# A list-scheduled attention and feed-forward kernel: new assumed durations and due times, plain reads for the unsplit products

## The chip, the cores and the metric

The kernel runs on one core of a Trainium2 chip. The metric is the time of one execution in microseconds (us), taken on the device; the median of some runs is compared. Engines are named as in the profile: PE is TensorE's matmuls, PEld its weight loads, DVE VectorE, ACT ScalarE, POOL GpSimd, SP SyncE, whose queue issues nearly all DMAs here.

## The reference

Eight batches of eight heads, 576 positions, head size 64; 32 packed rows per head read keys and values first, and the queries then read the packed rows. The attention's output, 4608 tokens by 512, goes through an ELU feed-forward of width 2048.

```python
def sm_attn(qq, kk, vv):
    s = scale * np.matmul(qq, kk.transpose(0, 1, 3, 2))
    s = s - np.max(s, axis=-1, keepdims=True)
    a = np.exp(s)
    a = a / (np.sum(a, axis=-1, keepdims=True) + 1e-09)
    return np.matmul(a, vv)
p_packed = sm_attn(p, k, v)                  # (8, 8, 32, 64)
out = sm_attn(q, p_packed, p_packed)         # (8, 8, 576, 64)
x = out.transpose(0, 2, 1, 3).reshape(B * S, H * D)
h = x @ w_in                                 # w_in: 512 x 2048
g = np.where(h > 0.0, h, np.exp(np.minimum(h, 0.0)) - 1.0)
return g @ w_out                             # w_out: 2048 x 512
```

## The kernel before, in words

The kernel never forms x: since x = a @ p_packed, it multiplies p_packed by w_in first (tile `m`, `mstep`, line 814) and then the softmax weights `a` by `m` (lines 1049, 1311, 1318).

Work comes in **visits**: one batch, one of two windows of its tokens (256 or 320 columns), and a run of the 16 slices f of the hidden width. One slice of a visit is: product h on PE; `relu` and `exp` on ACT (1326 and 1332 or 1061 and 1064); `elu` on DVE (1335 or 1056), on the own 256 columns into `e`, on a window's odd 64 columns into `hb`, which is sent to DRAM and worked off at the end; a high part `g` (a cast, line 313) and the low rest (1349) of the result; and the product with w_out, on PE (1417 to 1420). Precise products are made from high and low halves in three passes at float32r. Only batches 0 and 1, for the first four slices, use one float32 product with nothing split (`h_whole`, line 1311); such a matmul stands in the trace as two records, and the order of the program shows it once. `in_turn` reads an operand's two halves alternately, one element of each; the host has ordered queries and w_out to suit.

From batch 2's second window on, the output product takes two slices at once in Strassen's form (`strassen_pair`): seven products of 256 columns in three passes each (21 matmuls of 256 columns, some against sums of w_out blocks that are loaded again from DRAM as `sw`), with sums of blocks on DVE (1131), a cast of 896 columns on ACT and its rest on DVE (1140). A pair that stands in `S_PLAINS` is made plainly instead: 12 matmuls of 512 columns (or their like in halves), 512-column cast and rest, no sums and no `sw`.

The weights come as 64-bit words and are **converted** in the first part of the run: for each of 32 slices of 512 KB a load into one of three `raw` buffers, two steps on ACT (`field` and `tail`, line 343), two on DVE (`size` 361, `signed` 371), and for w_out a cast and a rest (385).

All this is recorded as operations (`op`) with an urgency, the engines that can do it, an assumed duration on each, what it needs, and the buffers that it takes. `schedule()` then walks a clock of its own: whenever an engine is free, the most urgent ready operation goes to it. What comes out is only the **order** of the instructions on each engine; on the chip the engines follow it and wait for semaphores. SP's queue runs in order too, so a store that waits holds up the loads behind it. Urgencies are the number of the slice in the order of visits, less a lead: `LI` and `LO` for the conversion of w_in and w_out, `LM` for m, `T_ATT...` for six steps of a batch's attention, `TM...` for its m, `T_SL` for the loads of `sw`. `lag` is time that the walk adds after an operation before its result counts.

Of the kernel before, what the change touches and what calls it, by code (L numbers as in the profile page):

```python
# [14 lines left out]
AF = mybir.ActivationFunctionType  # L15
# [5 lines left out]
def packed_attention_elu_ffn(  # L21
# [29 lines left out]
    G = 2  # L51
# [28 lines left out]
    ]  # L80
    T_ATT = [11.5, 7.0, 12.0, 17.0, 11.5, 18.0]
    T_ATT1 = [-20.0, -19, -16.0, -3.0, -18.5, -9.5]
    LI = 5.0
    LO = 2.5
    LM = 2.0
    LOOK = 4.0
    TM = [22.0, 27.0, 34.5, 25.5]
    FIRST = "q i3 o2 i2 i0 v k i1 o0".split()
    T_S2 = -4.0
    STAY = 9  # L90
    SWITCH = 0.105
# [3 lines left out]
    T_WS = 21  # L95
    T_AS = 3
    S_PLAIN = []
    S_PLAINS = {
        (2, 0): [7], (2, 1): [0], (3, 0): [1], (3, 1): [0], (4, 0): [0], (4, 1): [1],
        (5, 0): [0], (5, 1): [0], (6, 0): [], (6, 1): [1, 7],  # L100
    }
    T_SW7 = 27
    T_ATTS = {3: [-4, 2, -1.0, 7, 13.0, 21.5], 4: [-1.5, 7, 13.5, 3.0, 12.0, 24.0], 5: [-3.0, -2, -8.5, -5.5, 14.5, 28.0], 6: [7, 9, 13.5, 1.5, 13.0, 24.5], 7: [-3.5, -6, -5, 7.5, 14.5, 22.0]}
    TMS = {3: [19, 29, 30.0, 30.5], 4: [22, 19.5, 26.0, 27.0], 5: [10.5, 29, 29.0, 31.0], 6: [23, 18.5, 26.0, 24.0], 7: [16.5, 35, 30.0, 31.0]}
    T_RL = 20.5
    T_RX = 1.5
    T_HS = 12.0
    S_FIRST = (2, 1)
    T_SW = 13.5
    T_SL = 10.0  # L110
    T_SE = 16.0
    LOOK_S = 5.5
# [66 lines left out]
    def schedule():  # L179
# [8 lines left out]
        todo = sorted(ops, key=lambda o: (o.prio, o.n))  # L188
        idle_at = {e: 0.0 for e in GAP}
        now, out, mode, converted = 0.0, [], None, 0  # L190
        conv = set(conv_ops)

        def engine_for(o):

            if o.wait or o.ready > now:
                return None
            for r in {id(b.ring): b.ring for b in o.take}.values():
                if not r.grant([b for b in o.take if b.ring is r], now):
                    return None

            spare = 2.0 * (converted < len(conv_ops))
            e = min(o.on, key=lambda e: max(idle_at[e], now) + o.on[e] + spare * (e == "DVE"))
            return e if idle_at[e] <= now else None
# [128 lines left out]
    def weights(f, first, prio):  # L332
# [57 lines left out]
        t = FIRST.index(name) - 60 if name in FIRST else prio - 8  # L390
        ld = op(t, {"DMA": 1.45}, load, take=[raw])
        x = op(prio, {"ACT": 0.66, "DVE": 0.42}, field, [ld], take=[mi_b], use=[raw])
        y = op(prio, {"ACT": 0.66, "DVE": 0.42}, tail, [ld], take=[rd_b], use=[raw])
        y = op(prio, {"DVE": 0.69}, size, [x, y], use=[mi_b, rd_b])
# [27 lines left out]
    def attention(b, ts):  # L422
# [85 lines left out]
        for name, fn, bufs, t in (  # L508
            ("k", load_k, k_b, ts[0] - 6), ("v", load_v, v_b, ts[0] - 5), ("q", load_q, q_b, ts[0] - 3),
        ):  # L510
            lds[name] = []
            if b == 0:
                t = FIRST.index(name) - 60
            for n, x in enumerate(bufs):
                prev_ld = op(
                    t, {"DMA": (3.3 if b < 3 else 3.8) / len(bufs)}, lambda e, fn=fn, n=n: fn(e, n),
                    take=[x] + ([p_b] if (name, n) == ("k", 0) else []), after=[prev_ld],
                    lag=1.5 * (b > 2),
                )
                lds[name].append(prev_ld)  # L520
# [84 lines left out]
        if b < S_FIRST[0] + 1:  # L605
            o1 = op(t, {"PE": 1.0}, s1, ld_k, take=ps1 + e1s, use=[p_b] + k_b, after=[free], mode=1)
            for g in range(G):
# [66 lines left out]

        o = op(ts[2], {"PE": 1.28}, pv, ld_v + tr_done, take=[ps, pp_b], use=v_b + e1T, mode=2)
        done = []
        for g in range(G):
            def norm(e, g=g, ps=ps):
                if e == "ACT":
                    nc.scalar.mul(pp_b.t[:, g, :], ps.t[:, g, :D], sv["ri"][:, g:g + 1])  # L680
                else:
                    nc.vector.tensor_scalar(
                        out=pp_b.t[:, g, :], in0=ps.t[:, g, :D], scalar1=sv["ri"][:, g:g + 1],
                        scalar2=None, op0=ALU.mult,
                    )

            done.append(op(
                ts[2], {"ACT": 0.25, "DVE": 0.27}, norm, [o, o5] + done,
                use=[ps, pp_b],
            ))  # L690
# [327 lines left out]
    def strassen_pair(i, b, win, f):  # L1018
# [57 lines left out]
        elif not half:  # L1076
            ps_b, h_b = banks(1), Buf(R["h"], lambda: None)
            x = op(
                i, {"PE": 0.714 * 2}, lambda e: [h_mm(ps_b.t[:, n * 2 * P:(n + 1) * 2 * P], n) for n in range(2)],
                need, take=[ps_b, h_b], use=m_b + [st.a], after=[run["h"]],  # L1080
# [8 lines left out]
        else:  # L1089
            done = []  # L1090
            for n in range(2):
                ps_b, h_b = banks(1), Buf(R["h"], lambda: None)
                e_b = ring_tile("e", work, [P, HT + 2 * P], F32, "e")
                x = op(
                    i + n, {"PE": 0.885}, lambda e, n=n, ps_b=ps_b: h_mm(ps_b.t[:, :n_tok], n),
                    need, take=[ps_b, h_b], use=m_b + [st.a], after=[run["h"]],
# [102 lines left out]
        for a, group in zip(acc, groups):  # L1199
# [14 lines left out]
            ns = [y[0] for _, y, _ in group if y[0] is not None]  # L1214
            cost = 1.386 if plain else 0.355 * len(group)
            run["out"] = op(
# [12 lines left out]
        if last:  # L1229
# [33 lines left out]
            q = i - T_SE  # L1263
            y = op(q, {"ACT": 0.37, "DVE": 0.4}, first, [acc[0].last], take=[part], use=acc[:1])
            y = op(q, {"DVE": 0.42}, add1, [y], use=[part, acc[0]])
# [19 lines left out]
    for i, (b, win, f) in enumerate(order):  # L1285
# [38 lines left out]

        def relu(e, ps_b=ps_b, e_b=e_b, n_tok=n_tok):
# [7 lines left out]

        def elu(out, cs, e_b=e_b, ps_b=ps_b):
# [22 lines left out]
        need_a = a_done[0 if (b % 2, win) == (0, 0) else 1]  # L1357
        cost = (1.07 if long else 0.87) if h_whole else (0.885 if long else 0.714)
        x1 = op(
# [37 lines left out]
        def out_mm(e, one=slice(0, 1), i=i, f=f, g_b=g_b, acc=acc, first=first, final=final, g_whole=g_whole):  # L1397
# [24 lines left out]
        prev_out = run["out"] = op(  # L1422
            i + LOOK, {"PE": (0.9 if g_whole else 0.693) * n_t}, out_mm,
            last + [w_split.get(f) if not g_whole and f < F_PLAIN else w_ready[False, f]]
# [5 lines left out]
        if final:  # L1430
            t0 = b * S + cols.start + HT * odd
            rows = [[t0, t0 + P], [t0 + P, t0 + 2 * P]]
            if i == len(order) - 1:

                outs = [prev_out, op(
                    i + LOOK, {"PE": 0.693}, lambda e: out_mm(e, slice(1, 2)), after=[prev_out],
                    use=[g_b] + acc,
# [89 lines left out]
```

## Time and profile before

| | us |
|---|---|
| Median of 3 runs (lowest, highest) | 694.3 (693.08, 696.58) |
| The profiled execution's own time | 692.21 |
| Its span, first to last instruction | 690.4 |
| PE busy in it | 656.0 |
| DVE busy in it | 589.3 |
| ACT busy in it | 452.6 |

The span is what the trace covers; 1.8 us of that execution lie around it. A busy PE is one with a matmul in its pipeline, so a PE that waits briefly between two matmuls still counts as busy.

### The profile page before, as it was taken

The numbers are of one execution on the slowest core, as the hardware profiler recorded it, in microseconds if no ns is written. First come the engines' busy times: TensorE is split into PE (matmuls) and PEld (weight loads), VectorE is DVE, ScalarE is ACT, GpSimd is POOL, SyncE is SP. The second block draws the span as 40 slices with busy tenths as digits, with TensorE's granted clock in tenths as the row PEclk, the third lists the DMA queues.
The fourth block names the chain that finished last, engine by engine and source line by source line (L and its number), as shares of the span: only waits on it lengthen the run. The fifth ranks groups of instructions, "written<-read, shape, count | busy, mean of one in ns | idle before, by whom it ended". The sixth has DMA issues, their size and how long they took to land.

```text
span 690.4 us, 15992 instructions
## 1 busy us (share of the span) xinstructions
PE 656.0 (95%) x6013; PEld 566.8 (82%) x6013; DVE 589.3 (85%) x1324; ACT 452.6 (66%) x897; POOL 18.4 (3%) x26
## 2 busy tenths in 40 slices
PE   7589998899999999999999999999999999999996
PEld 3356777677778879898879988898899988999996
DVE  4689888799999698878987898779998998878975
ACT  5678999975767467666565556665665666555541
POOL 0000011111121000000000000000000000000000
PEclk9899999999999999999999999999999999999999
DMA  9846578739578716879779976788789878676873
GB/s 324 301 131 230 167 226 211 163 94 280 163 201 227 274 40 204 276 229 332 248 225 319 309 246 209 244 275 314 248 281 328 282 228 247 208 219 179 282 230 129
DMA packets 99052, 160.95 MB, mean 233 GB/s; under 512 B 25760, under 2 KB 34976, under 8 KB 98720
## 3 DMA queue, kind: packets, MB, share of 16 engines
q1 hardware_dynamic: 96096, 154.70, 69.1%
q0 software_dynamic: 2880, 5.24, 5.0%
q8 instruction: 47, 0.77, 0.4%
q14 instruction: 29, 0.24, 0.1%
HBM read 132.64 MB, written 27.26 MB: 232 GB/s over the span
## 4 chain that ended last, share of the span: by engine, by line
PE 56%; DVE 24%; ACT 9%; DMA 7%; issue 3%; SPq 0%; DVEq 0%; ACTq 0%
PE psum L1205 29%; PE psum L1049 15%; DVE g L1140 3%; PE psum L814 2%; DVE m_lo L827 2%; DMA raw<-in_w_in 2%; ACT g L313 2%; DMA raw<-in_w_out 2%; DVE e L1335 2%; PE psum L1318 2%; DVE w L1131 2%; DVE w L1056 2%; DVE g L1349 1%; PE psum L1311 1%; PE psum L1417 1%
## 5 line engine op out<-in xcount | busy, mean ns | idle before, releaser
L1205 PE MATMUL psum<-sw,g 128*128 128x256 f32 x1140 | 165.9, 276 | 0.0
L1205 PEld LDWEIGHTS psum<-sw,g 128*128 128x128 f32 x1140 | 146.1, 192 | 8.8 <-issue 5.3
L313 ACT CAST g<-w 128x896 fp32r<-128x896 f32 (+1 forms) x88 | 79.8, 907 | 48.0 <-DVE w L1131 25.9
L1140 DVE TENSOR_TENSOR g<-w,g 128x896 fp32r<-128x896 f32 (+1 forms) x88 | 91.6, 1041 | 21.9 <-ACT g L313 21.7
L1049 PE MATMUL psum<-a_hi,m_hi 128*128 128x320 f32 (+1 forms) x352 | 104.6, 297 | 1.7 <-DVE hb L1056 0.7
L1049 PE MATMUL psum<-a_lo,m_hi 128*128 128x320 f32 (+1 forms) x352 | 101.4, 288 | 0.0
L1049 PE MATMUL psum<-a_hi,m_lo 128*128 128x320 f32 (+1 forms) x352 | 101.4, 288 | 0.0
L1131 DVE TENSOR_TENSOR w<-w 128x128 f32<-128x128 f32 (+1 forms) x237 | 79.0, 333 | 6.0
L1205 PE MATMUL psum<-wo_a,g 128*128 128x256 f32 (+1 forms) x510 | 82.7, 293 | 0.8 <-DVE hb L1056 0.6
L1049 PEld LDWEIGHTS psum<-a_hi,m_hi 128*128 128x128 f32 x352 | 67.0, 190 | 9.4 <-ACT e L1064 2.4
L1205 PEld LDWEIGHTS psum<-wo_a,g 128*128 128x128 f32 x510 | 69.9, 191 | 5.7 <-issue 2.0
L1061 ACT ACTIVATE e<-psum 128x320 f32<-128x320 f32 x96 | 41.5, 435 | 46.9 <-PE psum L1049 45.2
L1205 PE MATMUL psum<-wo_b,g 128*128 128x256 f32 (+1 forms) x477 | 71.6, 278 | 0.0
L1049 PEld LDWEIGHTS psum<-a_lo,m_hi 128*128 128x128 f32 x352 | 67.1, 191 | 0.2
L1049 PEld LDWEIGHTS psum<-a_hi,m_lo 128*128 128x128 f32 x352 | 67.0, 190 | 0.0
L1205 PEld LDWEIGHTS psum<-wo_b,g 128*128 128x128 f32 x477 | 62.2, 192 | 4.1 <-issue 3.9
L1056 DVE SCALAR_TENSOR_TENSOR w<-e,psum 128x256 f32<-128x256 f32 x96 | 39.7, 413 | 12.5 <-ACT e L1064 12.3
L1061 ACT ACTIVATE w<-psum 128x512 f32<-128x512 f32 x40 | 23.9, 598 | 40.2 <-PE psum L1049 21.1
L1064 ACT ACTIVATE e<-e 128x320 f32<-128x320 f32 x96 | 44.8, 471 | 2.6
L1326 ACT ACTIVATE e<-psum 128x256 f32<-128x256 f32 (+1 forms) x80 | 32.9, 412 | 19.1 <-PE psum L1318 14.4
L1318 PE MATMUL psum<-a_hi,m_hi 128*128 128x256 f32 (+1 forms) x128 | 38.0, 297 | 4.9 <-DVE hb L1335 2.2
L814 PE MATMUL psum<-w_in_sb,ppT 64*32 64x512 f32 (+1 forms) x640 | 37.2, 524 | 3.8 <-DVE w_in_sb L371 2.9
(123 smaller groups left out, 1284.5 us busy)
## 6 DMA issues: line engine op xcount, KB each, us to landing
sw<-sw_dram SPq DMA_DIRECT2D x316, 256.0 KB, 4.0
raw<-in_w_in SPq DMA_DIRECT2D x16, 512.0 KB, 4.4
raw<-in_w_out SPq DMA_DIRECT2D x16, 512.0 KB, 4.6
kvq<-in_v SPq DMA_DIRECT2D x16, 512.0 KB, 5.4
out<-part SPq DMA_DIRECT2D x32, 256.0 KB, 3.7
sw_dram<-sw SPq DMA_DIRECT2D x32, 256.0 KB, 3.7
kvq<-in_kT SPq DMA_DIRECT2D x14, 576.0 KB, 5.2
kvq<-in_qT SPq DMA_DIRECT2D x14, 576.0 KB, 6.5
```

The lines of the kernel that those rows point to most:

```text
L313: (nc.scalar.copy if e == "ACT" else nc.vector.tensor_copy)(out=out, in_=in_)
L814: nc.tensor.matmul(ps.t[cols_of(pair), g, :w], lhsT=st.ppT.t[rows_of(g), pair, :], rhs=w_in_sb[rows_of(g), pair, c * FC + part * w:c * FC ...
L827: nc.vector.tensor_tensor(out=m_b[1].t[:, :, fs], in0=ps.t[:, :, :w], in1=m_b[0].t[:, :, fs].bitcast(F32), op=ALU.subtract,)
L1049: nc.tensor.matmul(ps, lhsT=m_b[p].t[:, g, o:o + P], rhs=in_turn(st.a.t[q][:, g, cols]), start=(n == 0), stop=(n == 3 * G - 1),)
L1056: nc.vector.scalar_tensor_tensor(out=out, in0=e_, scalar=-1.0, in1=ps, op0=ALU.add, op1=ALU.max)
L1061: nc.scalar.activation(out=out, in_=ps, func=AF.Relu, scale=-1.0)
L1064: nc.scalar.activation(out=x, in_=x, func=AF.Exp, scale=-1.0)
L1131: nc.vector.tensor_tensor(out=out, in0=x, in1=y, op=o)
L1140: nc.vector.tensor_tensor(out=g_b.all[:, 7 * P:(7 + b1 - b0) * P], in0=blocks(b0, b1), in1=g_b.all[:, :(b1 - b0) * P].bitcast(F32), op=ALU ...
L1205: nc.tensor.matmul(a.t[:, at * H:(at + rhs.shape[1]) * H], lhsT=operand(blk, p), rhs=rhs, start=new and n == k == 0, stop=a.final == (u, m ...
L1318: nc.tensor.matmul(ps_b.t[:, :n_tok], lhsT=m_b[x].t[:, g, o:o + P], rhs=in_turn(st.a.t[y][:, g, cols]), start=(n == 0), stop=(n == 3 * G - 1),
L1326: nc.scalar.activation(out=e_b.t[:, :n_tok], in_=ps_b.t[:, :n_tok], func=AF.Relu, scale=-1.0)
```

## The change

It replaces numbers that only `schedule()` reads: assumed durations (the 320-column product h from 0.885 to 0.817 us, a group of an output product from 0.693 to 0.649, `field` and `tail` from 0.66 to 0.68 and 0.71), and a `lag` of 1.8 us for weight loads and of 1.5 us for the loads of batches 1 and 2, so that the walk counts their data as there later. It replaces all leads, the order of the first nine loads (`FIRST`), and the pairs made plainly: of those listed in `S_PLAINS` for Strassen windows 17 instead of 9. Last, the unsplit products of line 1311 read their operand in one piece instead of in turn; relu and elu then read PSUM by halves in turn, so that what they write has the same order as before.

```diff
-    LI = 5.0
-    LO = 2.5
-    LM = 2.0
+    LAG_W = 1.8
+    SPARE = 1.375
+    LI = 10.75
+    LO = 3.625
+    LM = 4.5
...
-    FIRST = "q i3 o2 i2 i0 v k i1 o0".split()
+    FIRST = "i3 q k i1 o2 i2 v i0 o0".split()
...
-        (5, 0): [0], (5, 1): [0], (6, 0): [], (6, 1): [1, 7],
+        (6, 0): [6],
+        (6, 1): [0, 1, 5, 6, 7],
...
-        ld = op(t, {"DMA": 1.45}, load, take=[raw])
+        ld = op(t, {"DMA": 1.5}, load, take=[raw], lag=0.0 if t < -55 else LAG_W)
...
-                    lag=1.5 * (b > 2),
+                    lag=1.5 * (b > 0),
...
-                        rhs=in_turn(st.af.t[:, g, cols]), start=(g == 0), stop=(g == G - 1),
+                        rhs=st.af.t[:, g, cols], start=(g == 0), stop=(g == G - 1),
...
+        def pairs(x, h_whole=h_whole):
+            return x.rearrange("p (i m) -> p i m", m=2) if h_whole else x
...
+            return x.rearrange("p (m i) -> p i m", m=2)[:, cs.start // 2:cs.stop // 2]
...
-                out=e_b.t[:, :n_tok], in_=ps_b.t[:, :n_tok], func=AF.Relu, scale=-1.0
+                out=pairs(e_b.t[:, :n_tok]), in_=h(slice(0, n_tok)), func=AF.Relu, scale=-1.0
...
-                out=out, in0=e_b.t[:, cs], scalar=-1.0, in1=ps_b.t[:, cs], op0=ALU.add, op1=ALU.max
+                out=pairs(out), in0=pairs(e_b.t[:, cs]), scalar=-1.0, in1=h(cs),
+                op0=ALU.add, op1=ALU.max,
```

What the new numbers do to the order is seen at three places. The first is SP's queue after the queries of batch 1 (`kvq<-in_qT`); `raw` are weight loads, `out<-part` the first stores of the output. Before:

```order
L502 DMA kvq<-in_qT 128x4x288 x2
L348 DMA raw<-in_w_in 128x1024
L1466 DMA out<-part 128x512
L1003 DMA rest_dram<-hb 256x1x64
```

And now (line 348 has become 371, 1466 has become 1500, 1003 has become 1026):

```order
L525 DMA kvq<-in_qT 128x4x288 x2
L371 DMA raw<-in_w_in 128x1024 x2
L371 DMA raw<-in_w_out 128x1024
L1026 DMA rest_dram<-hb 256x1x64
L1500 DMA out<-part 128x512
```

Three weight loads instead of one stand ahead of the first store.

The second is ACT's queue at the same time, where the visit of batch 0's long window begins (`e<-psum 128x320` is its first relu). Before:

```order
L313 CAST g<-e 128x256
L1332 ACTIVATE e<-e 128x256
L313 CAST a_hi<-k 128x2x288
L737 ACTIVATE tmp<-tmp 128x576
L1326 ACTIVATE e<-psum 128x320
L1332 ACTIVATE e<-e 128x320
L313 CAST g<-e 128x256 x2
```

And now (313 has become 336, 343 has become 366, 737 has become 760, 1326 and 1332 have become 1359 and 1365):

```order
L1365 ACTIVATE e<-e 128x256
L1359 ACTIVATE e<-psum 128x320
L1365 ACTIVATE e<-e 128x320
L336 CAST g<-e 128x256
L366 ACTIVATE mi<-raw 128x512
L366 ACTIVATE rd<-raw 128x512
L336 CAST g<-e 128x256
```

A weight's two conversion steps now stand among the casts of that visit. Counted over the whole order, 28 conversion steps stand ahead of the ninth relu where 21 did, 32 for 28 ahead of the 13th, 40 for 38 ahead of the 21st, 59 for 61 ahead of the 37th; all 64 stand ahead of the 41st in both.

The third is PE's queue in batch 3, second window, third pair, one of the eight that are now plain. Before, after the pair's last h matmul:

```order
L1205 MATMUL psum<-wo_a,g 128x256 x3
L1205 MATMUL psum<-sw,g 128x256 x3
L814 MATMUL psum<-w_in_sb,ppT 32x512 x8
L1205 MATMUL psum<-sw,g 128x256 x6
L1205 MATMUL psum<-wo_a,g 128x256 x6
L1205 MATMUL psum<-sw,g 128x256 x3
```

And now (1205 has become 1228):

```order
L1228 MATMUL psum<-wo_a,g 128x512 x12
```

21 matmuls of 256 columns are 12 of 512, and none reads `sw`. Counted over the program, PE's 256-column output matmuls are 144 fewer and its 512-column ones 84 more; DVE's sums (1131) are 24 fewer and 8 of its rests are 512 columns wide for 896; SP issues 32 loads of `sw` fewer. ACT's count of conversion steps is the same. Two more moves are told in words: batch 1's first scores (line 531, now 554) stand between the two halves of batch 0's first m on PE instead of behind both, and batch 2's first scores and their transposes stand some 65 and 35 us of PE work earlier. The last 100 rows of PE's and DVE's queues hold the same kinds of work as before.

## Rows read from the trace of the kernel before

**Rows 1.** The page: each engine's busy time in us, share of the span, and instructions.

```profile
PE 656.0 (95%) x6013; PEld 566.8 (82%) x6013; DVE 589.3 (85%) x1324; ACT 452.6 (66%) x897; POOL 18.4 (3%) x26
```

**Rows 2.** Stretches: length, PE, PEld, DVE, ACT, POOL busy (records), clock, DMA share, GB/s.

```profile
0.00:20.00 20.00, 13.93 (x169) 7.21 (x177) 8.50 (x17) 11.09 (x22) 0.70 (x6) 0.91 0.92 334
20.00:40.00 20.00, 12.77 (x209) 7.37 (x194) 16.52 (x35) 15.36 (x35) 0.00 (x0) 0.83 0.75 254
45.00:50.00 5.00, 5.00 (x34) 3.48 (x34) 4.97 (x12) 3.56 (x9) 0.00 (x0) 1.00 0.00 0
90.00:100.00 10.00, 8.98 (x48) 7.15 (x47) 8.34 (x19) 9.94 (x23) 1.35 (x2) 1.00 0.83 244
120.00:130.00 10.00, 7.32 (x42) 6.00 (x42) 7.44 (x17) 8.56 (x21) 1.76 (x2) 1.00 0.91 246
320.00:360.00 40.00, 38.77 (x386) 32.98 (x386) 38.85 (x70) 23.99 (x37) 0.00 (x0) 1.00 0.78 255
```

**Rows 3.** The same view, 40 to 240 us as one stretch.

```profile
40.00:240.00 200.00, 188.62 (x1486) 148.42 (x1485) 178.27 (x420) 154.14 (x364) 17.75 (x20) 1.00 0.70 197
```

**Rows 4.** The chain that ended last, pieces of it: start, length, what.

```profile
10.50 10.06 DMA raw<-in_w_in
...
370.44 2.59 PE psum L1205 x12
...
668.28 14.75 PE psum L1205 x132
```

**Rows 5.** TensorE's waits, 0 to 40 us: for what, us in all, times, longest.

```profile
PE psum L642 <- ACT tmp L555: 5.1, 3, 2.3
PE psum L814 <- DVE w_in_sb L371: 2.9, 1, 2.9
```

**Rows 6.** SyncE's timeline: start, length, line, DMA.

```profile
38.27 0.56 SPq L348 DMA_DIRECT2D raw<-in_w_in  x1
53.40 0.35 SPq L1466 DMA_DIRECT2D out<-part  x1
```

**Rows 7.** SyncE's longest wait from 36 to 70 us: us in all, times, longest.

```profile
SPq L1466 <- ACT g L313: 14.9, 1, 14.9
```

**Rows 8.** TensorE's waits, 40 to 240 us.

```profile
PE psum L1318 <- DVE hb L1335: 2.2, 5, 0.7
```

**Rows 9.** TensorE's waits, 240 to 600 us.

```profile
PE psum L572 <- DVE m_lo L827: 1.3, 2, 1.1
```

**Rows 10.** VectorE's groups by line and shape: busy us, mean ns, idle before.

```profile
L1140 DVE TENSOR_TENSOR g<-w,g 128x896 fp32r<-128x896 f32 x79 | 85.5, 1082 | 21.1 <-ACT g L313 20.9
L1131 DVE TENSOR_TENSOR w<-w 128x128 f32<-128x128 f32 x158 | 45.4, 287 | 3.2
...
L1131 DVE TENSOR_TENSOR w<-w 128x256 f32<-128x256 f32 x79 | 33.6, 425 | 2.7
...
L361 DVE SCALAR_TENSOR_TENSOR mi<-mi,rd 128x512 uint32<-128x512 uint32 x32 | 22.0, 689 | 12.5 <-ACT rd L343 11.6 <-ACT mi L343 0.4
...
L371 DVE SCALAR_TENSOR_TENSOR mi<-raw,mi 128x512 uint32<-128x512 uint32 x16 | 12.0, 747 | 0.0
...
L1140 DVE TENSOR_TENSOR g<-w,g 128x512 fp32r<-128x512 f32 x9 | 6.2, 683 | 0.8 <-ACT g L313 0.8
```

**Rows 11.** TensorE's timeline: start, length, line, tiles, shape, records.

```profile
43.27 0.67 PE L814 MATMUL psum<-w_in_sb,ppT 64*32 64x256 f32 x16
...
49.83 1.51 PE L1311 MATMUL psum<-k,m_hi 128*128 128x320 f32 x4
...
70.42 1.24 PE L1311 MATMUL psum<-q,m_hi 128*128 128x256 f32 x4
...
204.02 1.09 PE L814 MATMUL psum<-w_in_sb,ppT 64*32 64x512 f32 x16
```

**Rows 12.** ScalarE's groups, two of them: busy us, mean ns, idle before.

```profile
L1064 ACT ACTIVATE w<-w 128x512 f32<-128x512 f32 x40 | 25.3, 632 | 1.0
...
L343 ACT ACTIVATE mi<-raw 128x512 f32<-128x512 f32 x32 | 24.4, 764 | 10.0 <-DMA raw<-in_w_in 7.2 <-DMA raw<-in_w_out 2.6
```

More of the change, by code (lines that the diff above doesn't have):

```diff
@@ L189, in schedule @@
         idle_at = {e: 0.0 for e in GAP}
+        idle_at["DMA"] = 0.7
         now, out, mode, converted = 0.0, [], None, 0
@@ L390, in weights @@
         t = FIRST.index(name) - 60 if name in FIRST else prio - 8
-        ld = op(t, {"DMA": 1.45}, load, take=[raw])
-        x = op(prio, {"ACT": 0.66, "DVE": 0.42}, field, [ld], take=[mi_b], use=[raw])
-        y = op(prio, {"ACT": 0.66, "DVE": 0.42}, tail, [ld], take=[rd_b], use=[raw])
+        ld = op(t, {"DMA": 1.5}, load, take=[raw], lag=0.0 if t < -55 else LAG_W)
+        x = op(prio, {"ACT": 0.68, "DVE": 0.42}, field, [ld], take=[mi_b], use=[raw])
+        y = op(prio, {"ACT": 0.71, "DVE": 0.42}, tail, [ld], take=[rd_b], use=[raw])
         y = op(prio, {"DVE": 0.69}, size, [x, y], use=[mi_b, rd_b])
@@ L605, in attention @@
         if b < S_FIRST[0] + 1:
-            o1 = op(t, {"PE": 1.0}, s1, ld_k, take=ps1 + e1s, use=[p_b] + k_b, after=[free], mode=1)
+            o1 = op(t, {"PE": 1.15}, s1, ld_k, take=ps1 + e1s, use=[p_b] + k_b, after=[free], mode=1)
             for g in range(G):
@@ L673, in pv @@
                         )
-        o = op(ts[2], {"PE": 1.28}, pv, ld_v + tr_done, take=[ps, pp_b], use=v_b + e1T, mode=2)
+        o = op(ts[2], {"PE": 1.36}, pv, ld_v + tr_done, take=[ps, pp_b], use=v_b + e1T, mode=2)
         done = []
@@ L687, in attention @@
             done.append(op(
-                ts[2], {"ACT": 0.25, "DVE": 0.27}, norm, [o, o5] + done,
+                ts[2], {"ACT": 0.31, "DVE": 0.27}, norm, [o, o5] + done,
                 use=[ps, pp_b],
@@ L1214, in strassen_pair @@
             ns = [y[0] for _, y, _ in group if y[0] is not None]
-            cost = 1.386 if plain else 0.355 * len(group)
+            cost = 1.3 if plain else 0.335 * len(group)
             run["out"] = op(
@@ L1263, in strassen_pair @@
             q = i - T_SE
-            y = op(q, {"ACT": 0.37, "DVE": 0.4}, first, [acc[0].last], take=[part], use=acc[:1])
+            y = op(q, {"ACT": 0.45, "DVE": 0.4}, first, [acc[0].last], take=[part], use=acc[:1])
             y = op(q, {"DVE": 0.42}, add1, [y], use=[part, acc[0]])
@@ L1332, in ex, with elu @@
             nc.scalar.activation(out=x, in_=x, func=AF.Exp, scale=-1.0)
-        def elu(out, cs, e_b=e_b, ps_b=ps_b):
+        def elu(out, cs, e_b=e_b, h=h, pairs=pairs):
             nc.vector.scalar_tensor_tensor(
-                out=out, in0=e_b.t[:, cs], scalar=-1.0, in1=ps_b.t[:, cs], op0=ALU.add, op1=ALU.max
+                out=pairs(out), in0=pairs(e_b.t[:, cs]), scalar=-1.0, in1=h(cs),
+                op0=ALU.add, op1=ALU.max,
             )
@@ L1357, in packed_attention_elu_ffn @@
         need_a = a_done[0 if (b % 2, win) == (0, 0) else 1]
[L1358 removed]
+        cost = (1.07 if long else 0.87) if h_whole else (0.817 if long else 0.668)
         x1 = op(
@@ L1435, in packed_attention_elu_ffn @@
                 outs = [prev_out, op(
-                    i + LOOK, {"PE": 0.693}, lambda e: out_mm(e, slice(1, 2)), after=[prev_out],
+                    i + LOOK, {"PE": 0.649}, lambda e: out_mm(e, slice(1, 2)), after=[prev_out],
                     use=[g_b] + acc,
```

65 lines of the change are left out of this document (44 added, 21 removed).

## Prediction, written before the changed kernel ran

> **What bounds the kernel now.** I read the page first, then the busy time by stretches, then the waits, and last the chain that ended last. PE is busy for 656.0 us of the span of 690.4 [rows 1], so 34.4 us of idle PE are all that a better order can give back; the rest can move only with PE's own work. The stretches say where the idle time lies. In the first 40 us PE is busy for 13.93 + 12.77 us [rows 2]: 13.3 us idle. From 40 to 240 us it is busy for 188.62 of 200 [rows 3]: 11.4 idle. That leaves 9.7 behind 240 us. Near the end 132 matmuls take 14.75 us [rows 4], 0.112 us each, without a gap: there PE alone is the bound, and no order helps. That piece ends at 683.0 us, so most of the 9.7 are the last sums and stores.
>
> The first 24 us belong to the loads. The chain holds one weight load for 10.06 us [rows 4], since it lands behind v and q, and PE waits for its conversion for 2.9 us [rows 5].
>
> From 40 to 240 us three engines take turns. From 45 to 50 us DVE is busy for 4.97 of 5 us, ACT for only 3.56, and the DMA engines move nothing [rows 2]. SP's queue shows why: after the load at 38.27 nothing is issued before 53.40 [rows 6], because the first store of the output stands next and waits 14.9 us for ACT [rows 7]. Later the conversions come in a heap: from 90 to 100 us ACT is busy for 9.94 of 10 and PE loses 1.02, from 120 to 130 PE loses 2.68 [rows 2]. PE's own waits there are for elu on DVE (`hb`, 2.2 us in five waits) [rows 8], whose input comes from relu and exp, which stand behind conversion steps on ACT. Behind 240 us DVE is the engine that still makes PE wait: 38.85 of 40 us busy from 320 to 360, while PE loses 1.23 [rows 2]; two waits for `m_lo` take 1.3 us [rows 9].
>
> **The change, part by part.**
>
> *Eight more plain pairs.* Twelve 512-column matmuls take 2.59 us [rows 4], 0.216 each. The order has 84 of these more and 144 of 256 columns fewer: 84 x 0.216 - 144 x 0.112 = 18.1 - 16.1, so PE gets 2.0 us more, on the path, since PE is the bound where they stand. DVE loses 24 sums and 8 wide rests: 8 x (2 x 0.287 + 0.425) + 8 x (1.082 - 0.683) [rows 10] = 8.0 + 3.2 = 11.2 us less. That is off PE's path except where PE waits for DVE. Bounds: nothing, and what idle time PE has between 240 us and that end, 9.7 less the larger part of 7.4, some 4 us. I take 1.0 us, near the low end, because the waits by name are short [rows 9]. The 32 loads that fall away (256 KB each) free DMA time that nothing waits for by name; I count nothing, and it would cost nothing were it not so.
>
> *Unsplit products in one piece.* A run of four records at 320 columns takes 1.51 us, at 256 columns 1.24 [rows 11]: 0.27 us for 4 x 64 columns, 1.05 ns a column, read in turn. The m product reads w_in in one piece, also in float32, with eight small matmuls side by side, so that 16 records are two rounds: 1.09 us at 512 columns, 0.67 at 256 [rows 11], 0.42 us for 2 x 256 columns, 0.82 ns a column. The kernel has 32 records of each width, 18,432 columns: 18,432 x 0.23 ns = 4.2 us less on PE, between 32 and 79 us. If the in-turn read is not what makes the difference (the m matmuls use 64 rows, these 128), it is nothing. I take the row's price, but only 2.5 us of it for the end, since DVE is as full as PE there [rows 2] and will hold PE up for part of what it gains. For this, relu and elu now read PSUM by halves in turn. The nearest rows are conversion steps, which read every second word: on ACT 0.764 us for 512 columns against 0.632 for a plain read [rows 12], a fifth more; on DVE 0.747 against 0.689 [rows 10], a twelfth. On 16 relus of 0.4 us the fifth is 1.4 us of ACT's time; on 16 elus of 0.4 and 8 of 0.2 us the twelfth is 0.7 of DVE's; nothing at least. I take nothing, because ACT has gaps there [rows 2] and DVE's share is small.
>
> The Trainium skill, SBUF — State Buffer, section on the DMA port swizzle, speaks against this edit: it says that PSUM has lines of 8 bytes and that a pattern that is not contiguous there slows matmuls much. Here no matmul writes PSUM so, only reads by ACT and DVE become so; if DVE's were slowed by the fifth instead of the twelfth, the sum would be 1.7 us higher (0.2 x 8.2). No row before shows such a read of PSUM.
>
> *Earlier conversions, and loads ahead of stores.* The order puts three weight loads instead of one ahead of the store that blocked SP for 14.9 us, and 28 conversion steps ahead of the ninth relu instead of 21. So work moves out of the crowded stretch behind 90 us into the one from 45 to 60 us, where DMA and ACT have room. From 90 to 130 us PE loses the most; its idle time from 40 to 240 us is 11.4 us in all. Bounds: all of it, and, on the other side, 5.0 us lost: seven ACT steps are 3.5 weights, each with 0.689 + 0.747 us on DVE [rows 10] = 1.44, and DVE is full where they go [rows 2]. I take a gain of 4.5 us, 40% of the idle time, because ACT, not DVE, is the full one in the stretch that gets relief.
>
> *The first loads.* Both lists load the same things before the first product of m can begin: four slices of w_in, one of w_out, k, v, q. One w_in slice is the last in either. So the wait of 2.9 us [rows 5] stays; if that load came later still, each us would cost one. Batch 1's first scores now start between the two halves of m, and PE's three waits for their exp (5.1 us with batch 0's) [rows 5] can shrink. The longest is 2.3. Between nothing and that I take 0.8, since the loads still set the pace.
>
> *Assumed durations* cost nothing by themselves: no instruction changes with them. The end of the queues holds the same work, so the last stores stay.
>
> **The sum**, against the profiled execution's 692.2 us: + 2.0 - 1.0 - 2.5 - 4.5 - 0.8 = 685.4, that is 6.8 less. The median of the runs is 694.3, 2.1 above that execution; I predict the median, 694.3 - 6.8 = 687.5.
>
> **The rivals.**
>
> *A wash.* DVE is the bound up to 240 us: its 178.27 busy us of 200 [rows 3] leave no more room than PE's. Then neither the quicker products nor the conversions' new place reach the end, and there remain + 2.0 - 1.0 - 0.8: 694.5. The full DVE from 45 to 50 us speaks for it, ACT's full stretch from 90 to 100 us against it [rows 2].
>
> *Slower by early conversions.* The seven steps brought forward queue ahead of elu on DVE at 45 to 60 us, the h buffers come free later, PE waits, and what is lost is not given back because PE is then the bound: 692.2 + 2.0 - 1.0 - 0.8 + 5.0 = 697.4, as a median 699.5. It decides once PE's idle time between 40 and 240 us rises above some 16 us. For it: DVE's 4.97 of 5. Against it: PE is never idle there from 45 to 50 us [rows 2], and all 64 steps stand ahead of the 41st relu in both orders, so what DVE does early it need not do late.
>
> *Dearer PSUM reads*, the case of the page's rule: 1.7 us more on a full DVE, 689.2.
>
> **How the numbers follow.** A measurement of this kernel tells a change from none at about 0.5%, 3.5 us: faster is below 690.8, slower above 697.8. The forecast 0.55, with its own range 680 to 690.8; dearer PSUM reads 0.08, faster too; the wash 0.22; slower by early conversions 0.15. So faster 0.63, same 0.22, slower 0.15. The range must reach over the wash, and downward to where two thirds of the idle time before 240 us go (3.0 more), all 4.2 us of the unsplit products count (1.7 more) and the start gives its 2.3 (1.5 more): 681.3, and a little lower, for idle time behind 240 us. I give 679 to 697.
>
> **What would show it.** Records of the unsplit products 0.21 and 0.27 us apart instead of 0.27 and 0.34; relu on them still about 0.4 us. SP issuing weight loads between 39 and 53 us. ACT with gaps from 90 to 110 us, and PE's idle time from 40 to 240 us at 7 us or so. DVE's busy time some 11 us lower, PE's work 2 us lower in sum. The prediction is wrong if PE's idle time in that stretch does not fall, or if a new wait stands in batch 2's attention, whose first scores now come some 65 us of PE work earlier and hold their buffers that much longer.

## The result

The changed kernel takes 670.5 us (median of 4 runs, 670.38 to 671.9) where the kernel before takes 693.7 in the same rounds: a ratio of 0.966, 95% interval 0.964 to 0.969, or 23.2 us less. The forecast was 6.8 us less. Its profiled execution has a span of 668.7 us, 21.7 below that of before.

The page of the changed kernel, busy times and chain (as in [rows 1]):

```profile
PE 645.6 (97%) x5953; PEld 564.9 (84%) x5953; DVE 574.8 (86%) x1292; ACT 449.5 (67%) x905; POOL 18.5 (3%) x26
...
PE 83%; ACT 9%; DVE 3%; DMA 3%; issue 1%; DVEq 0%; ACTq 0%
```

PE's idle time, span less busy time, fell from 34.4 to 23.1 us; but its busy time fell too, by 10.4 us. The plain pairs cost 2.0 us and the products in one piece save 3.8 (below), so PE's own work explains 1.8 of these. The stretches that stand in [rows 2, 3], now:

```profile
90.00:100.00 10.00, 10.00 (x78) 8.63 (x62) 8.81 (x22) 10.00 (x24) 1.92 (x2) 1.00 0.66 185
120.00:130.00 10.00, 9.67 (x60) 8.57 (x59) 8.08 (x17) 9.97 (x25) 1.76 (x2) 1.00 0.87 204
320.00:360.00 40.00, 40.00 (x371) 36.15 (x374) 37.33 (x74) 26.15 (x44) 0.00 (x0) 1.00 0.75 249
40.00:240.00 200.00, 196.65 (x1582) 161.51 (x1582) 186.98 (x445) 163.84 (x392) 17.83 (x20) 1.00 0.71 202
```

From 40 to 240 us PE is idle for 3.4 us instead of 11.4. ACT is as full from 90 to 100 us as it was, fuller even, and PE loses nothing there. TensorE's waits of the changed kernel, 0 to 40 us and then 40 to 240 us (us, times, longest):

```profile
PE psum L837 <- DVE w_in_sb L394: 5.2, 1, 5.2
PE psum L665 <- ACT tmp L578: 4.0, 3, 2.1
```

```profile
PE psum L837 <- DVE m_lo L850: 1.0, 2, 0.7
PE psum L1341 <- DVE e L1368: 0.7, 2, 0.3
```

The waits for elu's `hb` [rows 8] are gone. In the first 40 us the three waits for exp, where the prediction looked for 0.8 us, have shrunk from 5.1 to 4.0 us [rows 5]. But the wait for the converted weights, which was to stay, has grown from 2.9 to 5.2, and PE's idle time there is 14.1 us where it was 13.3.

PE's timeline, runs of unsplit products at 320 and 256 columns, which took 1.51 and 1.24 us [rows 11]:

```profile
49.69 1.24 PE L1334 MATMUL psum<-k,m_hi 128*128 128x320 f32 x4
...
69.90 1.03 PE L1334 MATMUL psum<-q,m_hi 128*128 128x256 f32 x4
```

Eight runs of each kind save 8 x 0.27 + 8 x 0.21 = 3.8 us of PE, where the prediction had 4.2. Relu and elu on them, 40 to 77 us, read PSUM by halves now (before: 437, 402 and 200 ns on average for these three):

```profile
L1368 DVE SCALAR_TENSOR_TENSOR e<-e,psum 128x256 f32<-128x256 f32 x13 | 5.3, 405 | 0.0
L1368 DVE SCALAR_TENSOR_TENSOR hb<-e,psum 128x64 f32<-128x64 f32 x8 | 1.6, 204 | 0.0
```

```profile
L1359 ACT ACTIVATE e<-psum 128x320 f32<-128x320 f32 x8 | 3.5, 433 | 0.5 <-PE psum L1334 0.5
```

They are no dearer. The relus of batch 1's 256 columns, 72 to 80 us, do take 0.41 to 0.44 us where they took 0.37 to 0.40, but hardly for their reads: with plain reads in the new order (the first run below) they take 0.38 to 0.44, by halves in the order of before (the run with products in one piece alone) 0.37 to 0.39.

### The profile page after: what moved, and what is told of

Its sections match the earlier page's. It is cut to its first block, busy times and chain, and to the rows that moved or that the text cites. A ratio compares the mean times of both kernels' runs of the same rounds, so it can differ in the third digit from the quotient of the medians.

```text
span 668.7 us, 15793 instructions
## 1 busy us (share of the span) xinstructions
PE 645.6 (97%) x5953; PEld 564.9 (84%) x5953; DVE 574.8 (86%) x1292; ACT 449.5 (67%) x905; POOL 18.5 (3%) x26
## 4 chain that ended last, share of the span: by engine, by line
PE 83%; ACT 9%; DVE 3%; DMA 3%; issue 1%; DVEq 0%; ACTq 0%
PE psum L1228 38%; PE psum L1072 20%; PE psum L837 4%; PE psum L1341 4%; PE psum L1451 3%; PE psum L1454 3%; PE psum L1452 3%; ACT mi L366 2%; ACT e L1365 1%; ACT e L1359 1%; PE psum L736 1%; PE psum L691 1%; DMA raw<-in_w_in 1%; ACT g L336 1%; PE psum L665 1%
## 5 line engine op out<-in xcount | busy, mean ns | idle before, releaser
L1228 PE MATMUL psum<-sw,g 128*128 128x256 f32 x1044 | 149.4, 276 | 0.0
L1228 PEld LDWEIGHTS psum<-sw,g 128*128 128x128 f32 x1044 | 132.4, 192 | 6.0 <-issue 6.0
L1163 DVE TENSOR_TENSOR g<-w,g 128x896 fp32r<-128x896 f32 (+1 forms) x88 | 88.6, 1008 | 23.3 <-ACT g L336 23.1
L336 ACT CAST g<-w 128x896 fp32r<-128x896 f32 (+1 forms) x88 | 77.0, 876 | 44.5 <-DVE w L1154 19.9
L1228 PE MATMUL psum<-wo_a,g 128*128 128x256 f32 (+1 forms) x525 | 87.0, 298 | 0.0
L1228 PE MATMUL psum<-wo_b,g 128*128 128x256 f32 (+1 forms) x498 | 79.4, 289 | 0.0
L1228 PEld LDWEIGHTS psum<-wo_a,g 128*128 128x128 f32 x525 | 73.5, 191 | 4.3 <-issue 0.9
L1154 DVE TENSOR_TENSOR w<-w 128x128 f32<-128x128 f32 (+1 forms) x213 | 70.9, 333 | 5.3
L1228 PEld LDWEIGHTS psum<-wo_b,g 128*128 128x128 f32 x498 | 67.7, 191 | 5.2 <-issue 3.5
L336 ACT CAST m_hi<-psum 128x1024 fp32r<-128x1024 f32 (+1 forms) x36 | 31.2, 874 | 13.6 <-PE psum L837 11.7
```

The source lines that it names most:

```text
L336: (nc.scalar.copy if e == "ACT" else nc.vector.tensor_copy)(out=out, in_=in_)
L1154: nc.vector.tensor_tensor(out=out, in0=x, in1=y, op=o)
L1163: nc.vector.tensor_tensor(out=g_b.all[:, 7 * P:(7 + b1 - b0) * P], in0=blocks(b0, b1), in1=g_b.all[:, :(b1 - b0) * P].bitcast(F32), op=ALU ...
L1228: nc.tensor.matmul(a.t[:, at * H:(at + rhs.shape[1]) * H], lhsT=operand(blk, p), rhs=rhs, start=new and n == k == 0, stop=a.final == (u, m ...
```

## The experiments

Times are medians; ratios are to the kernel before in the same rounds, with 95% intervals. The theory at first was that the new **order** as a whole gives the gain, mostly by its leads; the rival was the **relief** of DVE by plain pairs.

### Parts of the change undone, one at a time

**Products in turn again**, in the order of the changed kernel:

```diff
-                        rhs=st.af.t[:, g, cols], start=(g == 0), stop=(g == G - 1),
+                        rhs=in_turn(st.af.t[:, g, cols]), start=(g == 0), stop=(g == G - 1),
...
```

(In the same edit relu and elu read PSUM plainly again.)

> The changed kernel, in the same order on every engine, with the unsplit products reading their operand in turn again (and relu and elu reading PSUM plainly). The trace of the changed kernel shows their records 0.216 and 0.269 us apart where they were 0.271 and 0.338 us, so PE's work here grows by 4.0 us between 32 and 79 us. Theory of the order (most of the 23 us come from the new order, and DVE is as full as PE in that stretch): 1 to 3 us slower than the changed kernel, 671.5 to 673.5 us, the last unsplit record 1 to 3 us later. Rival, PE is the bound there: all 4.0 us, 674.5. Rival, the order was fitted to the quicker products and falls apart without them: 677 or more, with new waits of PE before 80 us.

674.2 us, ratio 0.971 (0.968 to 0.974): 3.8 us slower than the changed kernel, nearest to the first rival: in the finished order the whole saving arrives.

**Plain pairs of before** (9 for 17):

```diff
-        (6, 1): [0, 1, 5, 6, 7],
...
+        (5, 0): [0], (5, 1): [0], (6, 0): [], (6, 1): [1, 7],
```

> The changed kernel with the nine plain pairs of before in place of its seventeen. PE's work falls by 2.0 us, DVE's rises by some 11 us. Theory of the order: the relief of DVE matters little, so the time is that of the changed kernel within 3 us, 668.5 to 673.5. Rival, relief: DVE's 11.2 us less work is what took away PE's waits behind 240 us; then they come back, the stretch from 240 to 600 us has 6 us or more of lost PE time again, and the time is 675 us or more.

673.4 us, ratio 0.971 (0.968 to 0.974): 2.9 us slower, though PE has 2.0 us less to do. That is just inside the first theory's bounds, but if these 2.0 us count in full, relief is worth 4.9 us, so the truth lies between the two. One wait that the changed kernel does not have stands in TensorE's waits of this one, 540 to 668 us:

```profile
PE psum L1220 <- DVE hb L1071: 1.4, 1, 1.4
```

**Leads of the first stage as before, and of the later stage as before:**

```diff
-    LI = 10.75
+    LI = 5.0
...
-    FIRST = "i3 q k i1 o2 i2 v i0 o0".split()
+    FIRST = "q i3 o2 i2 i0 v k i1 o0".split()
```

```diff
-    T_RL = 5.5
+    T_RL = 20.5
...
-    T_SL = 18.125
+    T_SL = 10.0
```

> The changed kernel with the leads of the first stage as before: conversion of w_in and w_out, batch 0's m, batch 1's attention, the first loads, and the four numbers that go with them. Theory of the order: the gain of 14 us up to batch 3's first Strassen product (244.4 to 230.4 us) hangs on these numbers; most of it goes, 9 us or more, so 680 us or above, with PE idle for 8 us or more of the stretch from 40 to 240 us (3.4 in the changed kernel, 11.4 in the one before). Rival: the assumed durations and later landings did it, whatever the leads: within 3 us of the changed kernel, 667 to 673.

> The changed kernel with the leads of the later stage as before: the attention and m of batches 2 to 7, the loads of sums and of the last rows, the leads of the Strassen windows. Theory of the order: behind 240 us the change gained about 7 us; with the old leads 4 to 8 of these go, 674 to 679 us, and up to 240 us the time is that of the changed kernel within 2 us, but for batch 2's attention. Rival, relief of DVE by the plain pairs gained those 7 us whatever the leads: 669 to 672.

680.7 us (0.980, 0.978 to 0.983), so 10.2 slower; and 675.7 us (0.972, 0.969 to 0.976), 5.2 slower. Both are as the theory of the order had them, but for the idle time of the first: it is 6.7 us from 40 to 240 us. The four parts undone add up to 22.1 of 23.2 us, which looked like a full account. It was not.

**Only the leads of the conversions as before:**

```diff
-    LI = 10.75
-    LO = 3.625
+    LI = 5.0
+    LO = 2.5
```

> The changed kernel with only the leads of the conversion of w_in and w_out as before (5.0 and 2.5 slices for 10.75 and 3.625). Theory that earlier conversions are what relieved the stretch from 90 to 155 us: 4 us or more slower than the changed kernel, 674.5 or more, PE's idle time from 80 to 160 us back from 1.1 to 3 us or more. Rival, the rest of the first stage's numbers did it (m, batch 1's attention, first loads): within 2 us, 668.5 to 672.5.

682.6 us (0.984, 0.982 to 0.987): 12.1 slower, more than with all first leads undone, which contain these two. PE's idle time from 80 to 160 us, which was to be 3 us or more, is 1.5, so the loss isn't where the theory put it. Nor does the edit undo the early conversions: 28 conversion steps still run ahead of the ninth relu on ACT, as they do in the changed kernel and with all first leads undone. The prices of undone parts don't add up: what such a run measures is in good part the misfit of what is undone to what stays.

### Parts done alone in the kernel before

**All new durations and landings, nothing else:**

```diff
-        ld = op(t, {"DMA": 1.45}, load, take=[raw])
+        ld = op(t, {"DMA": 1.5}, load, take=[raw], lag=0.0 if t < -55 else LAG_W)
...
-                    i + n, {"PE": 0.885}, lambda e, n=n, ps_b=ps_b: h_mm(ps_b.t[:, :n_tok], n),
+                    i + n, {"PE": 0.817}, lambda e, n=n, ps_b=ps_b: h_mm(ps_b.t[:, :n_tok], n),
...
-            cost = 1.386 if plain else 0.355 * len(group)
+            cost = 1.3 if plain else 0.335 * len(group)
...
-            i + LOOK, {"PE": (0.9 if g_whole else 0.693) * n_t}, out_mm,
+            i + LOOK, {"PE": (0.9 if g_whole else 0.649) * n_t}, out_mm,
```

> The kernel before, its leads, pairs and reads as they were, with only the new assumed durations, landings and the two rules of the walk that go with them. Each of the four parts undone by itself cost 3.8 (reads), 2.9 (pairs), 10.2 (first stage's leads) and 5.2 us (later stage's leads), 22.1 together, of 23.2 us between the medians. Theory of parts that add up: what is left for the durations alone is 1 us, so 691.5 to 694. Rival, truer durations make a better order whatever the leads: 4 us or more off, 690 or less. Rival, leads were fitted to the durations, so the old leads with new durations fit nothing: 697 or more, slower than the kernel before.

676.7 us, ratio 0.977 (0.974 to 0.979): 17.3 us faster than the kernel before, three quarters of the whole gain, with the leads, pairs and reads of before. The theory of parts that add up falls; the first rival holds. The page of this kernel has as many matmuls as [rows 1]:

```profile
PE 649.3 (96%) x6013; PEld 564.9 (84%) x6013; DVE 586.4 (87%) x1318; ACT 449.3 (67%) x903; POOL 18.5 (3%) x26
```

The same 6013 matmuls keep PE busy for 6.7 us less. In a span of 674.3 us its idle time is 25.0.

**The new leads of the first stage beside them** (pairs, reads and later leads of before):

> The kernel before with the new assumed durations and the new leads of the first stage, but the pairs, reads and later stage's leads of before. Theory of parts that add up: 670.5 + 2.9 + 3.8 + 5.2 = 682.4, so 680.5 to 684.5, and 10 us below the kernel with new durations alone. Rival, the first stage gains only beside the new pairs and reads: 686 or more.

678.2 us (0.979, 0.976 to 0.981): no gain over the durations alone. Both theories missed.

**Products in one piece, alone** (the first diff above, turned round, in the kernel before):

> The kernel before, in its own order, with only the unsplit products' operand read in one piece (and relu and elu reading PSUM by halves). PE's work falls by 4.0 us between 32 and 79 us. Theory that PE is the bound in that stretch whatever the order: 3 to 4 us faster than the kernel before, 690 to 691. Rival, as the prediction had it, DVE holds PE up in the order of before: 2.5 us or less, 691.2 to 694.

692.9 us (0.999, 0.997 to 1.001): at most 2 us of the 3.8 arrive, as the prediction had it for the order of before. That it is DVE that takes the rest was not tested.

### Which durations

The twelve of the engines; all that concerns loads; PE's eight of the twelve; the lags alone; then ACT's four:

```diff
-        x = op(prio, {"ACT": 0.66, "DVE": 0.42}, field, [ld], take=[mi_b], use=[raw])
-        y = op(prio, {"ACT": 0.66, "DVE": 0.42}, tail, [ld], take=[rd_b], use=[raw])
+        x = op(prio, {"ACT": 0.68, "DVE": 0.42}, field, [ld], take=[mi_b], use=[raw])
+        y = op(prio, {"ACT": 0.71, "DVE": 0.42}, tail, [ld], take=[rd_b], use=[raw])
```

> The kernel before with only the new assumed durations of the engines: eight of PE (the 320-column product h 0.885 to 0.817, an output group 0.693 to 0.649, 0.355 to 0.335 and so on) and four of ACT. All new durations and landings together made it 17.3 us faster. Theory A: PE's rows in the trace are 0.136 us a matmul of 320 columns (six make 0.817), 0.216 of 512 (three make 0.649), 0.112 of 256 (three make 0.335), so the old numbers had PE 7% slower than it is, and the walk left the other engines later than PE needs them; then this kernel keeps 12 us or more, 682 or less. Theory B: it is the loads' later landing; then this one is within 4 us of the kernel before, 690 or more. In between, both.

> The kernel before with only what concerns loads in the walk: a weight load 1.5 for 1.45 us, a lag of 1.8 us behind it, of 1.5 us behind the loads of batches 1 and 2, the DMA queue free from 0.7 us on, and 1.375 us for 2.0 as what a conversion step on DVE is counted dearer. Theory A (PE's durations): within 4 us of the kernel before, 690 or more. Theory B (landings): 12 us or more faster, 682 or less.

> The kernel before with only PE's eight new durations. Theory A: nearly all of what the engines' durations give, 12 us or more faster, 682 or less. Rival, ACT's four durations (conversion steps 0.68 and 0.71 for 0.66, norm 0.31 for 0.25, the first step of a store 0.45 for 0.37) matter as much, since ACT is the full engine from 80 to 120 us: 686 or more here.

> The kernel before with only the lags: 1.8 us behind weight loads (and 1.5 for 1.45 us each) and 1.5 us behind the loads of batches 1 and 2. Theory B: most of what all load numbers give, within 3 us of that kernel. Theory A: within 4 us of the kernel before.

> The kernel before with only ACT's four new durations (conversion steps 0.68 and 0.71 for 0.66, norm 0.31 for 0.25, a store's first step 0.45 for 0.37). PE's eight and ACT's four together gave 14.5 us, PE's eight alone 10.4. If the two add up, 3 to 5 us faster than the kernel before, 688 to 690.5; if ACT's only help beside PE's, within 2 us of it.

| new in the kernel before | us | ratio (95%) |
|---|---|---|
| engines' twelve | 678.5 | 0.979 (0.976 to 0.982) |
| loads: durations, lags, the rules with them | 694.2 | 1.002 (1.000 to 1.004) |
| PE's eight | 682.6 | 0.985 (0.982 to 0.988) |
| lags alone | 694.8 | 1.002 (1.000 to 1.004) |
| ACT's four | 693.5 | 1.001 (0.999 to 1.003) |

PE's eight durations alone give 10.4 us, a little less than the 12 that their theory asked for; ACT's four give nothing alone and some 4 beside PE's; the landings nothing alone and some 2 beside the others, which is within the noise. Six of PE's eight are those of products and became 6 to 8% shorter; the two of attention became longer (1.0 to 1.15 and 1.28 to 1.36 us). No run has the six or the two alone.

The run with the landings also tests the prediction's largest term. SyncE's timeline of it, from 36 us:

```profile
40.52 4.42 SPq L351 DMA_DIRECT2D raw<-in_w_in  x2
48.82 2.32 SPq L351 DMA_DIRECT2D raw<-in_w_out  x2
52.51 0.58 SPq L1006 DMA_DIRECT2D rest_dram<-hb  x1
53.30 1.13 SPq L1469 DMA_DIRECT2D out<-part  x2
```

Four weight loads stand ahead of the first store, and 29 conversion steps run ahead of the ninth relu on ACT, where before has 21 and the changed kernel 28. That is the move for which the prediction counted 4.5 us, and PE is busy for 188.92 us from 40 to 240 us, against 188.62 [rows 3]. In two stretches it does matter. Before, and then in this run:

```profile
60.00:70.00 10.00, 9.50 (x63) 5.92 (x62) 8.33 (x19) 8.80 (x18) 0.00 (x0) 1.00 0.72 230
90.00:130.00 40.00, 34.66 (x213) 28.21 (x211) 32.45 (x72) 37.60 (x84) 5.43 (x6) 1.00 0.86 223
```

```profile
60.00:70.00 10.00, 6.54 (x31) 3.11 (x29) 9.15 (x19) 7.24 (x15) 0.00 (x0) 0.83 0.80 236
90.00:130.00 40.00, 37.03 (x228) 30.92 (x229) 32.02 (x74) 38.92 (x86) 5.42 (x6) 1.00 0.79 193
```

From 90 to 130 us, where the prediction looked for relief, PE loses 2.4 us less. From 60 to 70 us it loses 3.0 us more, in one wait for batch 1's m on DVE:

```profile
63.74 0.67 PE L817 MATMUL psum<-w_in_sb,ppT 64*32 64x256 f32 x16 [3.13 <-DVE m_lo L830]
```

Three conversion steps run on DVE in the 4 us ahead of that `m_lo`. So gain and loss cancel, as far as these stretches tell. With PE's eight durations, on the other hand, 22 steps run ahead of the ninth relu, PE loses only 1.3 us from 90 to 130 us (busy for 38.68), and the time falls by 10.4 us. Early conversions are neither enough for the gain nor needed for it.

### Truth, shorter is better, or a lottery

```diff
-            cost = 1.386 if plain else 0.355 * len(group)
+            cost = 1.495 if plain else 0.3852 * len(group)
```

> The kernel before with PE's eight durations 1.15 times the new ones (the old ones are 1.07 times them, but for two of attention). Theory of truth (the nearer the walk's clock is to the chip's, the better its order; 1.07 gives 693, 1.0 gives 682.6): slower than the kernel before, 698 or more. Rival, lottery (any change of numbers shuffles the order, and the time falls anywhere): 682 to 692 is as likely.

> The kernel before with PE's eight durations 0.9 times the new ones, so 10% shorter than the trace has them. Theory of truth: slower than with the new ones, 687 or more. Rival, the shorter PE is counted, the sooner the other engines' work is put in, whatever is true: 682 or less. Lottery: anywhere from 676 to 695.

| PE's durations in the walk | us | ratio (95%) |
|---|---|---|
| 1.15 times the new | 714.9 | 1.033 (1.030 to 1.036) |
| of before, 1.06 to 1.08 times the new (the two of attention 0.87 and 0.94) | 692.7 | 1 |
| the new | 682.6 | 0.985 (0.982 to 0.988) |
| 0.9 times the new | 694.5 | 1.002 (1.000 to 1.005) |

The new ones are what the trace has: matmuls of 512 columns 0.216 us apart, three of which make an output group's 0.648; 0.112 at 256 columns [rows 4], three of which make 0.336. Of four points the one nearest to the trace is the best, and it gets worse both ways, by 32 us for 15% more. "Shorter is better" falls. A lottery had other bounds for the first of these runs; but its wide ones for the second hold, and it would put four points in such an order (least at the new ones, and rising from there with longer ones) once in eight times. It is unlikely, not excluded.

TensorE's waits from 40 to 240 us show what changes when PE is counted too slow. The longest for elu with 1.15, and then with the new ones:

```profile
PE psum L1318 <- DVE hb L1335: 3.0, 5, 0.8
PE psum L1318 <- DVE e L1335: 2.2, 4, 0.9
PE psum L1417 <- DVE hb L1335: 2.2, 3, 1.4
```

```profile
PE psum L1318 <- DVE e L1335: 0.5, 1, 0.5
...
PE psum L1311 <- DVE hb L1335: 0.3, 1, 0.3
```

All waits for elu together are 7.7 us, and 1.0; before, they are 5.8. The conversion steps that ACT runs ahead of the 37th relu are 64, 61 (before), 58 and, at 0.9, 54. A reading that fits, though no run tests it by itself: with a slow PE the walk believes that ACT and DVE have time for more of other work between two products than they have, elu comes late, and PE waits in many small pieces. Conversions are not all of that work, since the landings alone also put 64 steps ahead of the 37th relu, at the time of before. At 0.9 the conversions come late instead: the last one on DVE starts at 155.8 us, 14 later than before. From 240 to 600 us PE is then idle for 10.1 us against 4.1 with the new ones; why was not traced.

### Where the last 6 us come from

**New durations with products in one piece; with the new pairs too (the changed kernel with all old leads); and the changed kernel with reads and pairs of before:**

```diff
-    LI = 10.75
-    LO = 3.625
...
+    LI = 5.0
+    LO = 2.5
...
-    T_SL = 18.125
...
+    T_SL = 10.0
...
```

```diff
-        (6, 1): [0, 1, 5, 6, 7],
...
+        (5, 0): [0], (5, 1): [0], (6, 0): [], (6, 1): [1, 7],
...
-                        rhs=st.af.t[:, g, cols], start=(g == 0), stop=(g == G - 1),
+                        rhs=in_turn(st.af.t[:, g, cols]), start=(g == 0), stop=(g == G - 1),
```

> The kernel before with all new durations and landings and the unsplit products in one piece; leads and pairs of before. The first alone gave 676.7. The walk counts these products 1.07 and 0.87 us in both kernels; in turn they take 1.35 and 1.09, in one piece 1.08 and 0.86. Theory of truth: now that the order fits, the 4.0 us less on PE arrive: 672.5 to 674. Rival, DVE holds PE up there as in the order of before, where one piece alone gave 1.1 us: 675 to 677.

> The changed kernel with the leads of both stages as before: new durations, products in one piece and new pairs stay. With the new durations alone the kernel takes 676.7 us, with one piece beside them 677.7; undone alone in the changed kernel, the reads cost 3.8 us, the pairs 2.9, the first stage's leads 10.2, the later stage's 5.2. Theory of a fitted set: the leads, reads and pairs give something only together, so this kernel is no better than with the new durations alone, 675 to 680. Rival, the leads are what is left: 670.5 plus 10.2 plus 5.2, 684 or more. Rival, the pairs alone are worth their 2.9 here too: 673 to 675.

> The changed kernel with reads in turn and the pairs of before: new durations and new leads stay. Undone one at a time the two cost 3.8 and 2.9 us. If these add up, 676 to 678.5, which is the time of the new durations alone, and the new leads by themselves give nothing. Rival, the leads give something without them: 675 or less. Rival, they were fitted to the reads and pairs: 679.5 or more.

677.7 (0.978, 0.976 to 0.980), 677.9 (0.977, 0.975 to 0.980) and 676.1 us (0.974, 0.971 to 0.976). The first misses both of its forecasts, that of truer durations (672.5 to 674) by far. With the new durations in all four:

| | reads and pairs of before | new reads and pairs |
|---|---|---|
| leads of before | 676.7 | 677.9 |
| new leads | 676.1 | 670.5 |

Neither the leads nor the reads and pairs give anything measurable by themselves; together they give 6.2 us. With all new durations and landings and the old leads, whichever the reads, PE's unsplit products wait 2.2 us for batch 1's `q` on DVE; with the new leads this wait is gone. Quicker products don't help beside it: with one piece PE's idle time from 40 to 240 us is 7.1 us for 5.4, and behind the wait the granted clock falls (0.66 from 65 to 70 us in that trace, 1.00 without one piece), which costs some 1.7 us by estimate (5 x 0.34). The wait of 1.4 us for `hb` shown above stands in all kernels here that have PE's new durations and the old pairs (one with 1.6), and in none with the new pairs: this is what DVE's relief takes away. That much of the fit is seen; the rest was not traced to single waits, and why the new leads need both edits stays open.

## Why the prediction was wrong

**The step that failed** is "Assumed durations cost nothing by themselves: no instruction changes with them". No instruction changes, but the order does, and by the run with the durations alone that is 17.3 of the 23.2 us; PE's eight numbers alone are 10.4. PE waits less in that order: its idle time falls from 34.4 to 25.0 us, and its busy time from 656.0 to 649.3. The numbers were on the page of the change and beside them in the trace: 0.693 for what takes 3 x 0.216, 0.885 for six matmuls of 320 columns that PE's timeline has 0.137 us apart. The change's side was read as a number that no instruction carries, and not laid beside the trace.

**"34.4 us of idle PE are all that a better order can give back"** failed too. With the same matmuls and the new durations, idle time fell by 9.4 and busy time by 6.7 us. PE's timeline of the kernel before shows how a wait hides in a busy engine (start, length, and in brackets the idle time that the view counts):

```profile
122.09 0.59 PE L1420 MATMUL psum<-wo_b,g 128*128 128x512 f32 x2
123.40 0.35 PE L1318 MATMUL psum<-a_hi,m_hi 128*128 128x256 f32 x1 [0.71 <-DVE hb L1335]
...
125.00 0.59 PE L1420 MATMUL psum<-wo_b,g 128*128 128x512 f32 x2
125.44 0.27 PE L1318 MATMUL psum<-a_hi,m_hi 128*128 128x256 f32 x1
```

Without a wait the next product starts 0.44 us after the start of the pair ahead of it, with one 1.31 us after: 0.87 us are lost, and 0.71 count as idle. The other 0.16 lie under the end of the pair, whose record runs on for 0.15 us after the next could start. A short wait of this kind costs that much more than it shows, and one below 0.16 us would show nothing. The sum agrees: against the usual spacing of each kind of matmul (those of 64 rows left out), starts behind 40 us come 14.3 us less late in the run with the durations alone than before, by an estimate from the two traces, and 7.6 of these count as idle; the other 6.7 are the fall in busy time.

**Early conversions, 4.5 us.** The stretch gained more than that (8.0 us of idle time), but not by this move in itself: the run with the landings makes it, gains 2.4 us from 90 to 130 us, loses 3.0 from 60 to 70, and is no faster. That loss is of the kind that the prediction had as its rival, conversion steps on DVE ahead of what PE needs. Nor was the reading of [rows 8] whole: one line has 2.2 us of waits for elu, all lines of that view together have 5.8. The sign that was named, ACT with gaps from 90 to 110 us, did not come. Of the reason given, that a crowded ACT makes PE wait, the changed kernel shows the opposite: ACT is busy for 10.00 of 10 us from 90 to 100 us beside a PE that is never idle. What counts, then, is rather whether relu and elu come in time among the conversions.

**Plain pairs, +2.0 and -1.0.** PE's part was right. DVE's relief was sized at 1.0 from the waits by name and is some 4.9 in the changed kernel, of which one wait of 1.4 us is seen; with the old leads the pairs give nothing.

**Products in one piece, 2.5 of 4.2 us.** The size on PE was right (3.8), and so was the doubt that it would arrive in the order of before, whether or not DVE is the reason: alone at most 2 us arrive, beside the new durations alone none, in the full set 3.8.

**First loads, 0.8 us.** Half right: the waits for exp shrank by 1.1 us, but the wait that was to stay grew by 2.3, and PE's idle time before 40 us grew by 0.8.

**The rivals.** A wash and a loss by early conversions did not come. Nor did dearer reads of PSUM: relu takes 433 ns by halves and 437 plainly, elu 405 and 402. The Trainium skill, SBUF — State Buffer, section on the DMA port swizzle, has patterns that are not contiguous in PSUM slow matmuls; for reads by ACT and DVE these rows show no such price. (By its own terms, 0.2 x 8.2, that rival was 1.6 us, not 1.7.)

## What to carry to other kernels

Where a list schedule walks a clock of its own, first compare its assumed durations of the bounding engine with the spacing of that engine's instructions in the trace; durations of which most were some 7% too long cost 10 us here, and nothing but two numbers in two texts had to be laid side by side. Calibrate before leads are chosen, and price leads and the edits chosen beside them together: undone one at a time they added up to a full account that was wrong. Take an engine's idle time as a lower bound of what waits cost it, when its records overlap.

## What was not expected of the hardware

A wait of PE can cost more than its length, when TensorE's clock falls behind it. In the changed kernel with the old leads of the first stage, PE waits 2.2 us for batch 1's `q` near 62 us (length, PE, PEld, DVE, ACT, POOL, clock, DMA share, GB/s):

```profile
60.00:65.00 5.00, 2.27 (x19) 1.36 (x20) 4.97 (x10) 3.54 (x6) 0.00 (x0) 0.74 0.93 299
65.00:70.00 5.00, 5.00 (x26) 2.80 (x24) 3.80 (x9) 3.35 (x8) 0.00 (x0) 0.58 0.52 187
```

After 2.7 us of idle time PE is busy for all of the next 5 us at a granted clock of 0.58, mostly at 1.2 GHz. The same wait does not always do it: with all leads as before, at a granted clock of 1.00, the twelve records behind it take 2.42 and 1.32 us, and here 6.35. These lines are from the timelines of that run and of this one:

```profile
63.13 2.42 PE L1322 MATMUL psum<-q,m_hi 128*128 128x320 f32 x8 [2.22 <-DVE q L774]
66.73 1.32 PE L1322 MATMUL psum<-q,m_hi 128*128 128x320 f32 x4 [1.18 <-DVE hb L1356]
```

```profile
63.40 6.35 PE L1334 MATMUL psum<-q,m_hi 128*128 128x320 f32 x12 [2.22 <-DVE q L786]
```

By this comparison some 2.6 of the 10.2 us that the first leads seemed to be worth are the clock's. In the kernel before and the changed one the clock is 1.00 from 40 us on, in every stretch shown. And a float32 product that reads its operand's two halves in turn, one element of each, takes a fifth longer than one that reads the same elements in one piece (a run of 1.51 us for 1.24, 1.24 for 1.03); the prediction had this only from different products.
